# A gated mix of two attentions: every score and maxima product on 30 rows, and a re-spread order of the local work

## The chip, the core and the metric

The kernel runs on one core of one Trainium2 chip. Its engines are the TensorE (PE in the profile, with its weight loads shown apart as PEld), the VectorE (DVE), the ScalarE (ACT), GpSimd (POOL) and the SyncE (SP), which issues nearly all DMAs. Each engine takes its instructions in the order in which the program wrote them. The metric is the device time of one execution in microseconds; a time given for a kernel is the median of its runs.

## The reference

The input `x` has 2048 rows of 448 numbers; there are 16 heads of 28 numbers each. Two attentions are computed from the same `x`, with weights of their own, and mixed row by row with a gate.

```python
g = _sigmoid((x * gate_w).sum(-1, keepdims=True))
# A: each position looks at itself and at 7 earlier ones, 2 apart
idx = pos[:, None] - off[None, :]                  # off = arange(8) * 2
logits = jnp.einsum("bhsd,bhswd->bhsw", q, kg) * scale
logits = jnp.where(mask[None, None, :, :], logits, -1e9)
attn = _softmax(logits, axis=-1)
o = jnp.einsum("bhsw,bhswd->bhsd", attn, vg)       # then @ wo
# B: full attention
scores = jnp.einsum("bhqd,bhkd->bhqk", q, k) * (Dh ** -0.5)
p = _softmax(scores, axis=-1)
o = jnp.einsum("bhqk,bhkd->bhqd", p, v)            # then @ wo
return g * a + (1 - g) * b
```

A is called the local attention below, B the full one.

## The kernel before

Products that need more precision than one rounded operand gives are made of three: each operand is held as a rounded high part and a low part (the rest), and high by high, high by low and low by high are summed in PSUM.

**Stages.** First the projections: q, k and v of both attentions, with the q and k of the full one stored to DRAM as high and low parts (`qk_hi`, `qk_lo`). Then the main loop, 256 steps. A step is numbered `st = 16 * u + kt`: `u` runs over 16 units (4 groups of 4 heads, by 4 blocks of 512 queries), `kt` over 16 tiles of 128 keys. Last the output projection.

**Tiles of the scores.** `KH` and `KL` hold the high and low part of the keys of one group, `QH` and `QL` those of the queries of one unit. The four heads of a group lie at partitions 0, 32, 64 and 96, 28 rows each, so that the products of four heads use four row groups of the array. Under the 28 rows of `QH` lie two more that hold minus the row maximum (its high and low part); `KH` was filled with ones at the start, so a product over 30 rows gives the score with its maximum already taken off. The products with a low part, `KH` by `QL` and `KL` by `QH`, use 28 rows.

**A step** (`scores`, L1016 to L1060, in the list `WITH`): for each of the four heads three products of 512 columns (term 0: `KH` by `QH` on 30 rows; term 1: `KH` by `QL`; term 2: `KL` by `QH`), 12 in all at L1042. Between them stand up to three products s0, s1, s2 at L149 (28 rows), which are the scores of a coming unit with the queries as stationary operand; the DVE takes their maxima over the keys (L155: one reduction of 512 columns for s0, one of 1024 for s1 and s2). These maxima are used up after step 234; the last 21 steps have 12 products (`ALONE`). Two exponentials a step (L1047, ACT, 128x1024) turn the scores into `P`, and eight products (L1008, `av`) add `P` by `V` of the step before.

**The banks.** Three pairs of PSUM banks rotate through a step: one for heads 1 and 2, one for heads 3 and 0, one for s1 and s2. The pair that s1 and s2 of a step wrote, and that the second maxima reduction reads, is in the next step the pair of heads 3 and 0. So the product called 30 below (head 3, term 0) waits for the second reduction of the step before.

**The local attention** is worked off beside the main loop in 8 chunks, from four lists of items (`item`, `issue`): POOL multiplies and adds, DVE reduces (L663 for the scores, L674 and L684 for maximum and sum, L687 the reciprocal, L720 the transposition of the result), ACT takes one exponential for each chunk (L679), SP loads and stores. What a step takes of them is set by a budget: `late[engine]` grows by the cost of each item taken and falls by `step`, the assumed length of a step in microseconds, after each. For the DVE it also grows by 0.6 for each maxima product. An item is taken when what it needs was issued some steps before and the budget is not over its limit; the DVE takes at most two small instructions a step.

**Other work with a fixed place in a unit:** `osb` (L905) copies the finished `av` out, `onhi` (L943) rounds a finished unit's output, at the start of the step with kt 15 for most units and of kt 0 and 2 for the first. These stand ahead of that step's exponentials in ACT's order; the local exponential stands behind them.

Of the kernel before, what the change touches and what calls it, by code (L numbers as in the profile page):

```python
# [8 lines left out]
F32 = mybir.dt.float32  # L9
F32R = mybir.dt.float32r  # L10
# [5 lines left out]
S, D, H, DH = 2048, 448, 16, 28  # L16
NB, NJ, NG = 4, 16, 4
W, DIL = 8, 2
HALO = (W - 1) * DIL
SCALE = DH ** -0.5  # L20
NU = NG * NB
NMX = 192
# [3 lines left out]
def gated_mix_kernel(ctx: ExitStack, tc: tile.TileContext, xT, xn, gw, wA, wB, woAB, out):  # L26
    nc = tc.nc
# [3 lines left out]
    qk_hi = dram.tile([2 * D, S], F32R, name="qk_hi")  # L31
    qk_lo = dram.tile([2 * D, S], F32R, name="qk_lo")
# [42 lines left out]

    QP = [[cp.tile([128, 512], F32R, name=f"QP{i}{k}") for k in range(2)] for i in range(2)]

    def init_kh(t):
        nc.gpsimd.memset(t.bitcast(F32), 1.0)

    def pair(name):
        return pp.tile([128, 2, 512], F32, tag="P", name=name)

    half = {}
# [16 lines left out]
            r = D + 112 * g + DH * h  # L105
            dma_r(t[32 * h:32 * h + DH, c], src[r:r + DH, c])

    def load_part(u, name, src):
        g, b = divmod(u, NB)
        t = sp.tile([128, 512], F32R, name=name)  # L110
        for h in range(4):
            r = 112 * g + DH * h
            dma_r(t[32 * h:32 * h + DH, :], src[r:r + DH, 512 * b:512 * b + 512])
        return t

    Qs = {}

    def load_q(u, low=True):
        Qs[u] = load_part(u, "QH", qk_hi), load_part(u, "QL", qk_lo)
        if low:  # L120
            load_nm(u)

# [18 lines left out]
    def s1_mm(n, bank, half=False):  # L141
        u, i = divmod(n, 64)
        qs, kc, h = i // 16, i // 4 % 4, i % 4
        if u == 0:
            qs, kc = i // 8 % 4, 2 * (i // 32) + i // 4 % 2
        if i == 0 and u + 1 < NU:
            load_qhi(u + 1)
        r = slice(64 * (h // 2), 64 * (h // 2) + 64) if half else slice(32 * h, 32 * h + DH)
        nc.tensor.matmul(bank, qhis[u][h % 2][r, 128 * qs:128 * qs + 128],  # L149
                         KH[u // NB % 3][r, 512 * kc:512 * kc + 512], start=True, stop=True)  # L150

# [56 lines left out]

    for t in KH:
        init_kh(t)  # L210
    t0 = pair("t0")[:, 0, :]
    nc.vector.memset(t0, 0.0)
    nc.vector.memset(zt, 0.0)
    nc.vector.memset(omt, 0.0)

    zero = nc.const_aps.tensor(0.0, [128, 512], F32).bitcast(F32R)

# [391 lines left out]
    def main_tiles():  # L609
        nonlocal mp, pm, maskt, actx, a1, a2, a3  # L610
        hctx.close()
        mp = ctx.enter_context(tc.tile_pool(name="mp", bufs=1))

        KH.append(mp.tile([128, S], F32R, name="KH2"))
        KL.append(mp.tile([128, S], F32R, name="KL1"))
        init_kh(KH[2])
        pm = ctx.enter_context(tc.tile_pool(name="pm", bufs=8))

        maskt = mp.tile([128, W, NJ, 2], F32, name="maskt")
        nc.gpsimd.memset(maskt, 0.0)  # L620
        for st, g, t, src in ((12, 2, KH[2], qk_hi), (30, 1, KL[1], qk_lo), (72, 2, KL[0], qk_lo),
                              (100, 3, KH[0], qk_hi), (136, 3, KL[1], qk_lo)):
            at("end", st, lambda g=g, t=t, src=src: load_k(g, t, src))
        for w in range(1, W):
            nc.gpsimd.memset(maskt[0:1, w, 0:DIL * w, :], -1e9 / SCALE)

        actx = ExitStack()
        a1 = actx.enter_context(tc.tile_pool(name="a1", bufs=1))
        a2 = actx.enter_context(tc.tile_pool(name="a2", bufs=2))
        a3 = actx.enter_context(tc.tile_pool(name="a3", bufs=5))  # L630
        for nme in ("k", "v"):
            for i in range(2):
                t = a1.tile([128, HALO + NJ, 56], F32, name=f"{nme}t{i}")
                kvt[nme, i] = t
# [155 lines left out]
    def issue(eng, st, limit):  # L790
        q = lists[eng]
        i = 0
        while i < min(len(q), LOOK):
            if eng == "dve" and small.get(st, 0) >= 2:
                return
            key, name, cost, needs, f = q[i]
            if any(d in names and issued.get(d, 10 ** 6) + lag > st for d, lag in needs):
                i += 1
                continue
            if eng in late:  # L800
                if late[eng] + cost > limit:
                    return
                late[eng] += cost
            counted(f) if eng == "dve" else f()
            issued[name] = st
            q.pop(i)
            i = 0
# [211 lines left out]
    def scores(u, kt, cur):  # L1019
# [9 lines left out]
        for tok in WITH if k else ALONE:  # L1029
# [8 lines left out]
                continue  # L1038
            a, t = tok[0], int(tok[1])
            h = (int(a) + n) % 4  # L1040
            r = slice(32 * h, 32 * h + (DH + 2 if t == 0 else DH))
            nc.tensor.matmul(bank[a], (KH[g % 3], KH[g % 3], KL[g % 2])[t][r, ks], (qh, ql, qh)[t][r, :], start=(t == 0), stop=(t == 2))  # L1042
            if t == 2 and a in "20":
                if len(exps) < 5:
# [12 lines left out]
    for u in range(NU):  # L1057
        g, b = divmod(u, NB)
        for kt in range(NJ):
# [29 lines left out]
                at("dve", st + lag, lambda t=t, w=turned: w.update(r=counted(lambda: max_turn(t))))  # L1089
                at("end", st + lag, lambda v=v, w=turned: max_store(v, w["r"]))  # L1090
            issue("dve", st, DLIM)
            issue("act", st, 0)
            run("act", st)
            if prev is not None:
                do_av(prev)
# [6 lines left out]
                accs.extend((ring[0][:, 0, :], ring[1][:, 0, :]))  # L1102
                op_mm(0, accs[0], (0, 1, 2), first=True)
            run("end", st)
            step = 2.2 if left else 2.1
            late["dve"] = max(0.0, late["dve"] + 0.6 * min(3, left) - step)
            late["pool"] = max(0.0, late["pool"] - step)
    do_av(prev)
# [33 lines left out]
```

## Time and profile before

| | |
|---|---|
| median of 3 runs | 896.43 us (896.38 to 896.9) |
| the profiled execution's own time | 896.69 us |
| its span, first to last instruction | 894.9 us |
| granted TensorE clock over the span | 1.000 |
| busy: PE, DVE, ACT, POOL | 890.2, 740.5, 642.4, 638.7 us |
| projections, to the main loop | 0 to 248.4 us |
| main loop | 248.4 to about 824 us |
| output projection | from 821.4 us, 71 us to the end |

The stretches follow from where the first instruction at L1042 and the first at L886 stand. Durations of the engines overlap: an instruction can begin about a tenth of a microsecond before the one ahead of it has ended, so busy time divided by the span overstates how full DVE and ACT are. The end of a matmul is modelled, so its start is the surer number, and the distance between the starts of two matmuls of one row group is what is read below.

### The profile page before, as it was taken

To read this page: it belongs to the slowest core of one execution; us is meant where nothing else is said; L and a number is where in the kernel's file an instruction comes from. 1 tells how busy PE (TensorE), PEld (TensorE's weight loads), DVE (VectorE), ACT (ScalarE), POOL (GpSimd) and SP (SyncE) were. 2 spreads that over 40 slices of the span, in tenths; PEclk is the share of its full clock that TensorE was granted. 3 is DMA by queue.
4 is the path that set the end of the run, shared out by engine and by line. 5 is a ranking of instruction groups with operands and counts; after the bars stand their busy time and mean duration, and the time that the engine had idled before them with its cause. 6 is when DMAs were issued, how large, how long until landed. Compare 5 with 4: busy or idle time off the path is not lost.

```text
span 894.9 us, 20516 instructions
## 1 busy us (share of the span) xinstructions
PE 890.2 (99%) x8312; PEld 533.4 (60%) x8312; DVE 740.5 (83%) x962; ACT 642.4 (72%) x766; POOL 638.7 (71%) x505
## 2 busy tenths in 40 slices
PE   9999999999999999999999999999999999999998
PEld 7889999999954444444444444444444444434997
DVE  6688999999979999999999999999999999832220
ACT  7456434343378898898988989989888898897220
POOL 1499846464459789998999989999999799701000
PEclk9999999999999999999999999999999999999999
DMA  8886403454372241225225222533121322437781
GB/s 267 277 267 186 151 12 84 135 142 121 103 248 66 89 139 46 67 61 156 71 56 143 86 62 86 128 96 98 45 64 32 89 43 49 104 78 214 192 265 52
DMA packets 114038, 104.51 MB, mean 117 GB/s; under 512 B 75240, under 2 KB 82280, under 8 KB 113160
## 3 DMA queue, kind: packets, MB, share of 16 engines
q1 hardware_dynamic: 113512, 102.42, 40.7%
q8 instruction: 65, 1.06, 0.5%
q10 hardware_dynamic: 432, 0.79, 0.3%
q14 instruction: 29, 0.24, 0.1%
HBM read 62.20 MB, written 40.96 MB: 115 GB/s over the span
## 4 chain that ended last, share of the span: by engine, by line
PE 99%; ACT 0%; issue 0%; ACTq 0%
PE T L1042 31%; PE av L1008 28%; PE r L325 15%; PE r L320 8%; PE T L886 8%; PE r L149 4%; PE T L149 4%; PE r L220 0%; PE av L472 0%; ACT P L1047 0%; ACT res L895 0%; ACT onhi L943 0%; ACT L L679 0%; ACTq L943 0%
## 5 line engine op out<-in xcount | busy, mean ns | idle before, releaser
L1047 ACT ACTIVATE P<-T 128x1024 f32<-128x1024 f32 x512 | 496.8, 1023 | 59.6 <-PE T L1042 57.9
L155 DVE TENSOR_REDUCE MX<-T 128x1 f32<-128x512 f32 x470 | 442.5, 954 | 31.7 <-PE T L149 13.7
L1008 PE MATMUL av<-P,V 128*32 128x512 f32 x2048 | 272.7, 605 | 0.0
L1042 PEld LDWEIGHTS T<-QH,KH 30*128 30x128 f32 x1024 | 92.2, 181 | 229.1 <-ACT P L1047 196.5
L149 PE MATMUL T<-KH,QP 28*128 28x512 f32 x704 | 220.3, 456 | 0.1
L1042 PE MATMUL T<-QH,KH 30*128 30x512 f32 x1024 | 211.7, 489 | 0.2 <-ACT P L1047 0.2
L171 DVE TENSOR_REDUCE MX<-r 128x2 f32<-128x1024 f32 x160 | 192.9, 1221 | 20.1 <-PE r L149 16.3
L1042 PE MATMUL T<-QH,KL 28*128 28x512 f32 x1024 | 185.7, 393 | 0.0
L1042 PE MATMUL T<-QL,KH 28*128 28x512 f32 x1024 | 184.3, 392 | 0.0
L653 POOL TENSOR_TENSOR prod<-qt,kt 128x896 f32<-128x896 f32 x64 | 135.4, 2116 | 6.4 <-DMA kt<-a_scr 6.4
L397 ACT ACTIVATE raw<-r 128x896 f32<-128x896 f32 (+1 forms) x62 | 57.1, 921 | 94.5 <-PE r L325 91.9
L149 PE MATMUL r<-KH,QP 64*128 64x512 f32 x320 | 114.5, 391 | 0.0
L714 POOL TENSOR_TENSOR oat<-oat,prod 128x896 f32<-128x896 f32 x48 | 101.2, 2109 | 2.0
L149 PEld LDWEIGHTS T<-KH,QP 28*128 28x128 f32 x704 | 86.1, 181 | 26.7 <-ACT P L1047 17.7
L325 PE MATMUL r<-wh,xh 64*128 64x448 f32 (+1 forms) x504 | 99.6, 363 | 0.0
L709 POOL TENSOR_TENSOR prod<-vt,L 128x896 f32<-128x896 f32 x56 | 95.3, 1702 | 0.3
L398 POOL TENSOR_TENSOR ast<-raw 128x448 f32<-128x448 f32 x47 | 54.3, 1154 | 56.4 <-ACT raw L397 43.9
L1042 PEld LDWEIGHTS T<-QL,KH 28*128 28x128 f32 x1024 | 94.3, 185 | 0.0
L1042 PEld LDWEIGHTS T<-QH,KL 28*128 28x128 f32 x1024 | 93.3, 183 | 0.2
L1008 PEld LDWEIGHTS av<-P,V 128*32 128x32 f32 x2048 | 40.3, 107 | 77.9 <-issue 65.4
L325 PE MATMUL r<-wl,xh 64*128 64x448 f32 (+1 forms) x441 | 79.0, 365 | 0.0
L325 PEld LDWEIGHTS r<-wh,xh 64*128 64x128 f32 x504 | 77.9, 185 | 0.1
(122 smaller groups left out, 1138.8 us busy)
## 6 DMA issues: line engine op xcount, KB each, us to landing
a_scr<-ast SPq DMA_DIRECT2D x24, 448.0 KB
qk_hi<-qkh SPq DMA_DIRECT2D x24, 256.0 KB
qk_lo<-qkh SPq DMA_DIRECT2D x24, 256.0 KB
rbc<-rs SPq DMA_DIRECT2D x64, 64.0 KB
QP<-qk_hi SPq DMA_DIRECT2D x64, 56.0 KB
KL<-qk_lo SPq DMA_DIRECT2D x16, 224.0 KB
QH<-qk_hi SPq DMA_DIRECT2D x64, 56.0 KB
QL<-qk_lo SPq DMA_DIRECT2D x64, 56.0 KB
```

The costliest lines, as they stand in the source:

```text
L149: nc.tensor.matmul(bank, qhis[u][h % 2][r, 128 * qs:128 * qs + 128], KH[u // NB % 3][r, 512 * kc:512 * kc + 512], start=True, stop=True)
L155: i = nc.vector.tensor_reduce(MX[:, n % NMX:n % NMX + k], bank, axis=X, op=ALU.max)
L171: nc.vector.tensor_reduce(m, PM[k], axis=X, op=ALU.max)
L320: nc.tensor.matmul(bank, ws[c][rows, k, t[4]:t[4] + 128], x, start=first, stop=last)
L325: nc.tensor.matmul(bank[:, 0:cols], x, ws[c][rows, k, 0:cols], start=first, stop=last)
L653: nc.gpsimd.tensor_tensor(out=p, in0=qt[c], in1=kvt["k", c % 2][:, HALO - DIL * w:HALO - DIL * w + NJ, :], op=ALU.mult)
L709: nc.gpsimd.tensor_tensor(out=dst.rearrange("p j (h d) -> p j h d", d=DH), in0=kvt["v", c % 2][:, HALO - DIL * w:HALO - DIL * w + NJ, :].r ...
L714: nc.gpsimd.tensor_tensor(out=ows[c % 2][:, :, 0:56] if w == W - 1 else oat[c], in0=oat[c], in1=oat[c, w], op=ALU.add)
L886: writes(bank, nc.tensor.matmul(bank[:, :D], src, wo[c][k], start=(first and k == ks[0] and i == 0), stop=(last and k == ks[-1] and i == 2)))
L1008: nc.tensor.matmul(av[32 * h:32 * h + 32, :], V[:, kt, 4 * g + h, :], tiles_[h], start=(kt == 0), stop=(kt == NJ - 1), skip_group_check=True)
L1042: nc.tensor.matmul(bank[a], (KH[g % 3], KH[g % 3], KL[g % 2])[t][r, ks], (qh, ql, qh)[t][r, :], start=(t == 0), stop=(t == 2))
L1047: e = nc.scalar.activation(p, one if a == "2" else mine, AF.Exp, scale=SCALE).ins
```

## The change

Five edits, shown in the diff. `ROWS` is 30. The products of terms 1 and 2 at L1042 and the maxima products at L149 that used 28 rows now use 30. So that the two added rows give nothing, `KL` is filled with zeros at the start (POOL), and `QL`, which was a tile of a rotating pool, becomes two fixed tiles filled with zeros (DVE); the added rows of `QP`, the queries of the maxima products, are zeros already. Loads into these tiles write the same 28 rows of each head as before.

In the order of the local work, `step` goes from 2.2 to 2.17 while there are maxima products, and the local exponential is not taken in steps with kt 14 or 0.

```diff
+ROWS = DH + 2
...
+    QL = [cp.tile([128, 512], F32R, name=f"QL{i}") for i in range(2)]
     QP = [[cp.tile([128, 512], F32R, name=f"QP{i}{k}") for k in range(2)] for i in range(2)]
...
+    def init_kl(t):
+        nc.gpsimd.memset(t.bitcast(F32), 0.0)
...
-    def load_part(u, name, src):
+    def load_part(u, t, src):
         g, b = divmod(u, NB)
-        t = sp.tile([128, 512], F32R, name=name)
...
-        Qs[u] = load_part(u, "QH", qk_hi), load_part(u, "QL", qk_lo)
+        Qs[u] = load_part(u, sp.tile([128, 512], F32R, name="QH"), qk_hi), load_part(u, QL[u % 2], qk_lo)
...
-        r = slice(64 * (h // 2), 64 * (h // 2) + 64) if half else slice(32 * h, 32 * h + DH)
+        r = slice(64 * (h // 2), 64 * (h // 2) + 64) if half else slice(32 * h, 32 * h + ROWS)
...
+    init_kl(KL[0])
     t0 = pair("t0")[:, 0, :]
     nc.vector.memset(t0, 0.0)
     nc.vector.memset(zt, 0.0)
     nc.vector.memset(omt, 0.0)
+    for t in QL:
+        nc.vector.memset(t.bitcast(F32), 0.0)
...
         init_kh(KH[2])
+        init_kl(KL[1])
...
-            r = slice(32 * h, 32 * h + (DH + 2 if t == 0 else DH))
+            r = slice(32 * h, 32 * h + ROWS)
...
-            issue("act", st, 0)
+            if kt not in (NJ - 2, 0):
+                issue("act", st, 0)
...
-            step = 2.2 if left else 2.1
+            step = 2.17 if left else 2.1
```

On PE no product is added, removed or moved; the numbers of the loads and stores on SP are the same. DVE gains two fills, POOL two. Three places where the order changes:

The DVE in the main loop, steps 156 to 158 (`MX<-T` 128x1 and 128x2 are the two maxima reductions of a step, `L<-prod` the reductions of local scores); before:

```order
L155 TENSOR_REDUCE MX<-T_3245 128x1
L155 TENSOR_REDUCE MX<-T_3237 128x2
L663 TENSOR_REDUCE L<-prod 128x16 x2
L155 TENSOR_REDUCE MX<-T_3245 128x1
L155 TENSOR_REDUCE MX<-T_3233 128x2
```

and now:

```order
L159 TENSOR_REDUCE MX<-T_3249 128x1
L159 TENSOR_REDUCE MX<-T_3241 128x2
L159 TENSOR_REDUCE MX<-T_3249 128x1
L159 TENSOR_REDUCE MX<-T_3237 128x2
L671 TENSOR_REDUCE L<-prod 128x16 x2
```

The pair of local reductions moved one step on. Of the first 233 steps, 68 had no small DVE instruction behind their maxima, 98 had one and 67 two; now it is 61, 112 and 60. All the small instructions that stood among steps with maxima products stand there still.

ACT around steps 110 to 113 (`P<-T` are the exponentials, `onhi<-on` and `osb<-av` the work with a fixed place, `L<-L` the local exponential); before:

```order
L1047 ACTIVATE P<-T_3237 128x1024
L679 ACTIVATE L<-L 128x256
L943 ACTIVATE onhi<-on 128x512
L1047 ACTIVATE P<-T_3241 128x1024
L1047 ACTIVATE P<-T_3233 128x1024
```

and now:

```order
L951 ACTIVATE onhi<-on 128x512
L1055 ACTIVATE P<-T_3245 128x1024
L1055 ACTIVATE P<-T_3237 128x1024
...
L1055 ACTIVATE P<-T_3241 128x1024
L913 ACTIVATE osb<-av 128x512
...
L687 ACTIVATE L<-L 128x256
```

The local exponential of this chunk stands two steps later, no longer right ahead of a rounding. That of the first chunk goes the other way: it stood a step ahead of the first half of a rounding and now stands right ahead of it, at the turn from step 31 to 32.

SP after the last maxima, steps 240 to 247 (`rs<-osb`, `fsum`, `rs<-finv`, `rbc` are the row sums of unit 14 going through DRAM, `oa_scr<-tw` the last chunk of the local result, `oar` its first load for the output projection); before:

```order
L726 DMA oa_scr<-tw 384x1x32
L910 DMA rs_14_82<-osb 4x512
L914 DMA fsum<-rs_14_82 128x16
L923 DMA rs_14_98<-finv 128x16
L928 DMA rbc<-rs_14_98 32x512 x4
L856 DMA oar<-oa_scr 128x512
```

and now:

```order
L918 DMA rs_14_82<-osb 4x512
L922 DMA fsum<-rs_14_82 128x16
L734 DMA oa_scr<-tw 512x1x32
L734 DMA oa_scr<-tw 384x1x32
...
L931 DMA rs_14_98<-finv 128x16
L734 DMA oa_scr<-tw 512x1x32
...
L936 DMA rbc<-rs_14_98 32x512 x4
L864 DMA oar<-oa_scr 128x512
```

Before, all eight stores stood ahead of `rs<-osb`; now four stand behind `fsum` and four behind `rs<-finv`.

## The prediction

> **What bounds the kernel now.** I read the page's span and chain first.
>
> ```profile
> span 894.9 us, 20516 instructions
> PE 99%; ACT 0%; issue 0%; ACTq 0%
> PE T L1042 31%; PE av L1008 28%; PE r L325 15%; PE r L320 8%; PE T L886 8%; PE r L149 4%; PE T L149 4%; PE r L220 0%; PE av L472 0%; ACT P L1047 0%; ACT res L895 0%; ACT onhi L943 0%; ACT L L679 0%; ACTq L943 0%
> ```
>
> The chain names PE almost throughout. That says little, since overlapping matmul durations leave no visible idle time. So I went to windows of the main loop, and to the row of the maxima reductions in the first of them, for the length of a step.
>
> ```profile
> 288.41:757.06 468.65, 468.46 (x4790) 195.23 (x4786) 443.90 (x635) 418.41 (x472) 433.41 (x306) 1.00 0.31 81
> 757.06:779.46 22.40, 22.40 (x236) 9.40 (x232) 19.35 (x23) 19.71 (x22) 19.67 (x12) 1.00 0.39 89
> L155 DVE TENSOR_REDUCE MX<-T 128x2 f32<-128x1024 f32 (+1 forms) x417 | 393.0, 955 | 24.5 <-PE T L149 10.4 <-PE T L1042 6.0
> ```
>
> The columns after the length are busy time (and instructions) of PE, PEld, DVE, ACT and POOL, the clock, and DMA. Two maxima reductions a step, 417 of them, make 208 steps in the first window: 468.65/208 = 2.253 us a step. The second holds ten steps at the end of the maxima: 2.240 us. DVE is busy 443.90/208 = 2.134 us a step in the first and 1.935 in the second, where there is next to no local work. So 0.199 us of local DVE work a step costs 0.013 us of step. The clock is 1.00 in both.
>
> Then two whole steps by the timeline, PE first, then PEld, then DVE.
>
> ```profile
> 579.18 0.50 PE L1042 MATMUL T<-QH,KH 30*128 30x512 f32 x2
> ...
> 579.41 0.49 PE L1042 MATMUL T<-QH,KH 30*128 30x512 f32 x1
> 579.51 0.40 PE L1042 MATMUL T<-QL,KH 28*128 28x512 f32 x2
> 579.53 0.39 PE L1042 MATMUL T<-QH,KH 30*128 30x512 f32 x1
> ...
> 579.75 0.40 PE L1042 MATMUL T<-QH,KL 28*128 28x512 f32 x2
> 579.76 0.39 PE L1042 MATMUL T<-QL,KH 28*128 28x512 f32 x1
> 579.98 0.41 PE L1042 MATMUL T<-QH,KL 28*128 28x512 f32 x1
> ...
> 580.32 1.06 PE L1008 MATMUL av<-P,V 128*32 128x512 f32 x8
> 581.32 0.50 PE L1042 MATMUL T<-QH,KH 30*128 30x512 f32 x2
> ...
> 581.71 0.50 PE L1042 MATMUL T<-QH,KH 30*128 30x512 f32 x2
> ...
> 582.05 0.40 PE L1042 MATMUL T<-QL,KH 28*128 28x512 f32 x2
> ...
> 582.28 0.41 PE L1042 MATMUL T<-QH,KL 28*128 28x512 f32 x2
> 582.62 1.06 PE L1008 MATMUL av<-P,V 128*32 128x512 f32 x8
> 583.61 0.50 PE L1042 MATMUL T<-QH,KH 30*128 30x512 f32 x2
> ```
>
> ```profile
> 579.41 0.18 PEld L1042 LDWEIGHTS T<-QH,KH 30*128 30x128 f32 x2
> 579.52 0.18 PEld L1042 LDWEIGHTS T<-QL,KH 28*128 28x128 f32 x1
> ...
> 581.71 0.18 PEld L1042 LDWEIGHTS T<-QH,KH 30*128 30x128 f32 x2
> ```
>
> ```profile
> 578.13 1.23 DVE L155 TENSOR_REDUCE MX<-T 128x2 f32<-128x1024 f32 x1
> ...
> 579.75 1.90 DVE L155 TENSOR_REDUCE MX<-T 128x1 f32<-128x512 f32 x2
> ```
>
> The two steps begin at 579.18 and 581.32, and take 2.14 and 2.29 us. What differs is when product 30 (head 3, term 0) may load its weights. The second reduction of the step before ends at 578.13 + 1.23 = 579.36, and the load comes at 579.41; a step later it ends at 579.75 + 1.90 = 581.65, and the load comes at 581.71. From product 30 on both steps run alike: 0.34 to term 1, 0.23 to term 2, 0.34 to `av`, 1.00 to the next step, 1.90 together. So a step is (end of the maxima reduction + 0.05 to 0.06, from the step's start) + 1.90: 0.23 + 1.91 and 0.39 + 1.90. PE sets the step together with the DVE reduction that frees product 30's banks. A step that begins late finds that reduction nearer its end, so lost time is half returned by the next; that is why local DVE work costs so little.
>
> **The rows.** The edit could pay only if a change from 28 to 30 rows inside a row group costs something, and the 0.34 beside the 0.23 looks like it: 0.33 to 0.34 follows the 30-row products at 579.18, 579.41 and 581.71, 0.23 a 28-row one. But the 30-row product at 579.53 is followed in its row group by the 28-row one at 579.76, after 0.23, the same as the 0.24 from the 28-row products at 579.51 to those at 579.75. What the slow cases share is a first product with duration 0.49 or 0.50: its weights are loaded only as it starts (579.41 beside 579.41, 581.71 beside 581.71). The one at 579.53 had its weights loaded 0.12 ahead and lasts 0.39. The difference, 0.11 us, is a weight load not hidden behind a wait, and the change leaves those waits where they are. A load lasts 0.18 with 30 rows and 0.18 with 28, a product with hidden load 0.39 with either. So 1024 + 1024 products at L1042 and 704 at L149 go to 30 rows at 0.00 each. Bounds: dearer by at most the 0.01 to which these rows are read, on the three products from product 30 to `av`, 0.03 x 234 = 7 us if the rounding hid the most each time, which I give no weight since 0.39 stands at both row counts; cheaper by at most 0.11 a step (below).
>
> [...]
>
> **The fills.** One fill of `QL`, 128x512, is like the one at 0.91 below, one of `KL` is half of the two of `KH`.
>
> ```profile
> 0.91 0.48 DVE L212 MEMSET t<- 128x512 f32 x1 [0.91 <-PEq L1134]
> 4.64 0.43 DVE L443 CAST xh<-V 128x512 fp32r<-128x512 f32 x1 [3.18 <-DMA V<-in_xT]
> 1.25 3.54 POOL L83 MEMSET KH<- 128x2048 f32 x2
> 30.26 2.00 POOL L235 TENSOR_TENSOR wl<-raw,wh 128x384 fp32r<-128x384 f32 x2 [25.47 <-ACT wh L234]
> 261.60 2.13 POOL L653 TENSOR_TENSOR prod<-qt,kt 128x896 f32<-128x896 f32 x1 [6.44 <-DMA kt<-a_scr]
> ```
>
> The two of `QL`, 0.96 us, go into DVE's wait of 3.18 for the first input; `KL0`, 1.77, into POOL's wait of 25.47; `KL1`, 1.77, into its wait of 6.44 at the start of the main loop. Cost 0; uncovered, all of them 4.5 us.
>
> **The local work.** Nothing of it leaves the steps with maxima: the same instructions, placed more evenly. All local DVE work together costs 0.013 x 234 = 3.0 us, so between -3.0 and +3.0 lies whatever a new placing can do. If the price hangs on the steps with two small instructions, which fall from 67 to 60, the gain is 3.0 x 7/67 = 0.3 us. I take that, near zero, because the sum of work is unchanged.
>
> **The exponentials.** One place shows the collision that the edit is about.
>
> ```profile
> 500.57 0.42 ACT L679 ACTIVATE L<-L 128x256 f32<-128x256 f32 x1
> 500.88 0.63 ACT L943 ACTIVATE onhi<-on 128x512 fp32r<-128x512 f32 x1
> 501.40 4.01 ACT L1047 ACTIVATE P<-T 128x1024 f32<-128x1024 f32 x4
> 500.02:502.47 2.45, 2.27 (x27) 0.94 (x23) 2.42 (x5) 2.45 (x5) 2.45 (x2) 1.00 0.25 29
> ```
>
> Local exponential and rounding stand together ahead of the scores' exponential, and the step takes 2.45 instead of 2.25: 0.2 us, removed once. In the changed order the first chunk's exponential now stands right ahead of half a rounding (256 columns instead of 512), so about 0.1 comes back. Net -0.1. With this edit and the last, the two ends are -3.1 and +3.1.
>
> **The tail.** The last local stores move behind the row sums on SP. What waits behind them is the load of the local result, and behind that the split that PE needs.
>
> ```profile
> 790.80 5.92 SPq L726 DMA_DIRECT2D oa_scr<-tw  x8
> ...
> 805.87 0.42 SPq L856 DMA_DIRECT2D oar<-oa_scr  x1
> 815.98 0.69 DVE L865 TENSOR_TENSOR oalo<-oar,oahi 128x512 fp32r<-128x512 f32 x1
> 821.40 0.67 PE L886 MATMUL T<-KH,oahi 128*128 128x448 f32 x2
> ```
>
> The third block's split ends at 815.98 + 0.69 = 816.67; PE begins with it and the blocks before at 821.40. The eight issues of 0.74 each could slip 4.7 us before anyone waits. Cost 0.
>
> **Sum.** 0 (rows) + 0 (fills) - 0.3 - 0.1 + 0 = -0.4 us: 896.3 for the profiled execution, whose own time of 896.69 is 1.8 over its span and 0.26 over the median of the runs shown; 896.0 as a median.
>
> **Rivals.**
>
> 1. The even placing earns the whole price of the local work: steps of 2.240 throughout, -3.0, and -0.1 on ACT: 893.3. For it: 98 to 112 steps with just one small instruction. Against: 60 of the 67 pairs remain, and a late reduction is half returned anyway.
>
> 2. The change of rows does cost the 0.11 that I put down to unhidden loads. Each step's chain has one, from product 30, and as many steps as have maxima products would lose it: 0.11 x 234 = 25.7, so 870.3. For it: every 0.33 or 0.34 between two score products in these steps does follow one of 30 rows. Against: 579.53 to 579.76.
>
> 3. Slower, by the tail. If the eight stores go only after the second trip of the row sums, the load of the local result comes as late as that trip plus 5.92 us of issues. It decides once that load slips by over 4.7 us beyond 805.87; a slip of 7 us, the 5.92 and the rest of a landing, would put 2.3 us on the forecast's 896.0: 898.3. For it: four stores now stand behind `rs<-finv`. Against: the row sums no longer wait for the eight stores, so that trip begins earlier.
>
> **Chances.** Forecast 0.56, rival 1 0.22, rival 2 0.08, rival 3 0.14. The forecast's own range is 894.8 to 897.2. The range for 8 in 10 reaches down past rival 1 and up to rival 3: 892.0 to 898.5; rival 2 and about half of rival 3 stay out. A difference within 0.2%, 1.8 us, counts as none, about what a measurement of this kernel can tell: rivals 1 and 2 are faster, 0.30; the forecast is the same, 0.56; rival 3 slower, 0.14.
>
> **What would show it.** Rows right: in the changed timeline 0.34 still follows every product whose load comes with its start, and 0.23 the others, though all have 30 rows; 0.23 in the former shows rival 2. Local work right: 2.25 a step over the same stretch; 2.24 is rival 1. Exponentials: the step at 500.02 near 2.25 and the one after step 31 about 0.1 longer. Fills: the waits before the first cast and the first local product shorter by 0.96 and 1.77. Tail: idle PE ahead of the first L894 product would show rival 3. I am wrong, beyond the rivals, if products on 30 rows take another time than 0.39 when their weights are there, or if a reduction of local scores now waits for POOL, which none does before.

## The result and the profile after

The change is slower: 900.25 us (898.48 to 901.17, 5 runs) against 896.47 for the kernel before, run beside it (896.38 to 896.94), a ratio of 1.0037 with a 95% interval of 1.0026 to 1.0048. Run again in a later job, it stood at 898.86 (896.71 to 900.84, 9 runs) against 896.76, ratio 1.0024 (1.0014 to 1.0034). So the loss is 2 to 4 us, 0.2 to 0.4%, and the change scatters over 2.7 and 4.1 us where the kernel before, run beside it, keeps within 0.7. The profiled execution of the change took 898.48 us with a span of 896.7, 1.8 more than before; it is the fastest of the first five, so it shows only a part of the loss.

The page's span and chain, as they were read first for the kernel before:

```profile
span 896.7 us, 20515 instructions
PE 95%; DMA 2%; SPq 2%; DVE 0%; ACT 0%; issue 0%
PE T L1050 29%; PE av L1016 27%; PE r L332 15%; PE r L327 8%; PE T L894 8%; PE T L153 4%; PE r L153 4%; DMA kt<-a_scr 1%; SPq L734 1%; SPq L105 1%; DMA V<-in_xT 0%; ACT P L1055 0%; PE av L479 0%; DVE xh L450 0%; DMA QH<-nm 0%
```

Before, the chain was PE for 99%. Now 4% of it are DMA and SP's queue, in names that were not in it: `kt<-a_scr` (a load of the local attention), L734 (the stores `oa_scr`), L105 (loads of queries), `QH<-nm` (the row maxima of the next unit), and `DVE xh L450`, the first cast of the program. These are what has to be explained.

The windows of the main loop, with the same columns as in the prediction; first the 208 steps and the ten behind them, then three single steps, 79, 159 and 111:

```profile
289.63:758.86 469.23, 467.72 (x4788) 194.89 (x4784) 443.56 (x632) 418.29 (x472) 424.87 (x301) 1.00 0.30 81
758.86:781.26 22.40, 22.40 (x233) 9.40 (x229) 20.48 (x27) 19.76 (x22) 21.17 (x14) 1.00 0.36 86
...
429.13:432.19 3.06, 2.26 (x29) 0.97 (x25) 2.86 (x6) 2.99 (x4) 2.98 (x3) 1.00 0.23 63
609.67:612.72 3.05, 2.34 (x28) 0.97 (x25) 2.62 (x5) 3.05 (x4) 2.97 (x3) 1.00 0.39 81
501.94:504.05 2.11, 2.11 (x27) 0.87 (x24) 1.99 (x4) 2.11 (x4) 2.11 (x2) 1.00 0.05 6
```

The stretch takes 0.58 longer than before, yet PE is busy 0.74 less: it stands idle 1.51 us, where it stood idle 0.19. The steps 79 and 159, each the last of a unit, take 3.06 and 3.05; before no step was longer than 2.46. Without their surplus over an ordinary 2.25 the stretch would be about 1.0 shorter than before. The last row is the step with the collision of exponentials (2.45 before): it now takes 2.11.

The stretch begins at 289.63 instead of 288.41, so 1.22 us were lost before it. The timeline from the start shows where: POOL's fills first, then DVE, then PE, and last PE's first real product in the kernel before.

```profile
1.25 3.54 POOL L85 MEMSET KH<- 128x2048 f32 x2
4.73 1.80 POOL L88 MEMSET KL<- 128x2048 f32 x1
```

```profile
1.51 1.03 DVE L221 MEMSET QL<- 128x512 f32 x2
4.48 2.34 DVE L450 CAST xh<-V 128x512 fp32r<-128x512 f32 x1 [1.94 <-DMA V<-in_xT]
```

```profile
0.77 4.60 PE L227 MATMUL r<-const-float32-0.0 128*128 128x512 f32 x10 [0.77 <-PEq L1143]
6.96 0.70 PE L327 MATMUL r<-xh,wh 128*128 128x512 f32 x2 [1.59 <-DVE xh L450]
```

```profile
5.22 0.71 PE L320 MATMUL r<-xh,wh 128*128 128x512 f32 x2
```

The two fills of `QL` went into DVE's wait, as forecast. The cast behind them took 0.43 before and takes 2.34 now. Read its end, not its start: before, POOL's last fill ended at 1.25 + 3.54 = 4.79 and the cast at 4.64 + 0.43 = 5.07, 0.28 later; now the last fill ends at 4.73 + 1.80 = 6.53 and the cast at 6.82, 0.29 later. The cast did not run beside that fill. It was held to its end, and PE's first real product, which was at 5.22 before, comes at 6.96. In all seven profiles with the third fill at the start, the cast ends at 6.81 or 6.82, wherever its record begins (4.48 to 4.72). What holds it no trace shows, and the recorded starts do not show the hold either: the cast's record begins at 4.48, ahead of the third fill's at 4.73, and its end still came behind that fill's.

The tail is as it was: from the start of step 240 to the end 105.53 us, before 105.56.

### The profile page after: what moved, and what is told of

Read it like the earlier page. It is cut to its first block, busy times and chain, and to the rows that moved or that the text cites. A ratio compares the mean times of both kernels' runs of the same rounds, so it can differ in the third digit from the quotient of the medians.

```text
span 896.7 us, 20515 instructions
## 1 busy us (share of the span) xinstructions
PE 889.1 (99%) x8312; PEld 532.8 (59%) x8312; DVE 748.5 (83%) x964; ACT 642.2 (72%) x766; POOL 642.9 (72%) x507
## 4 chain that ended last, share of the span: by engine, by line
PE 95%; DMA 2%; SPq 2%; DVE 0%; ACT 0%; issue 0%
PE T L1050 29%; PE av L1016 27%; PE r L332 15%; PE r L327 8%; PE T L894 8%; PE T L153 4%; PE r L153 4%; DMA kt<-a_scr 1%; SPq L734 1%; SPq L105 1%; DMA V<-in_xT 0%; ACT P L1055 0%; PE av L479 0%; DVE xh L450 0%; DMA QH<-nm 0%
## 5 line engine op out<-in xcount | busy, mean ns | idle before, releaser
L153 PE MATMUL T<-KH,QP 30*128 30x512 f32 x704 | 221.6, 460 | 0.1
L1050 PE MATMUL T<-QH,KL 30*128 30x512 f32 x1024 | 185.9, 393 | 0.0
L1050 PE MATMUL T<-QL,KH 30*128 30x512 f32 x1024 | 183.2, 388 | 0.0
L153 PEld LDWEIGHTS T<-KH,QP 30*128 30x128 f32 x704 | 86.1, 181 | 27.3 <-ACT P L1055 16.6
L1050 PEld LDWEIGHTS T<-QL,KH 30*128 30x128 f32 x1024 | 93.9, 184 | 0.0
L1050 PEld LDWEIGHTS T<-QH,KL 30*128 30x128 f32 x1024 | 93.0, 182 | 0.2
```

## The experiments

In the table, times are of the profiled executions, taken from the starts of the first score product of a step. "Loop" is step 2 to step 240 less the 534.84 of the kernel before; step 2 begins there at 254.51. "Against before" is the difference of the medians within one job, where both kernels ran on one chip.

| run | step 2 begins | step 79 | step 159 | loop | median | against before | ratio, 95% interval |
|---|---|---|---|---|---|---|---|
| the change | 255.82 | 3.06 | 3.05 | +0.49 | 900.25 | +3.78 | 1.0037 [1.0026, 1.0048] |
| e8_change_again | 257.22 | 2.15 | 2.96 | -0.54 | 898.86 | +2.10 | 1.0024 [1.0014, 1.0034] |
| e1_order_only | 254.28 | 2.70 | 2.79 | +0.61 | 897.67 | +0.96 | 1.0011 [1.0002, 1.0019] |
| e2_rows_only | 257.36 | 2.16 | 2.32 | -0.72 | 898.57 | +1.86 | 1.0014 [1.0005, 1.0023] |
| e3_fill_moved | 254.63 | 2.44 | 2.97 | -0.40 | 896.97 | +0.26 | 1.0003 [0.9994, 1.0011] |
| e4_early_load | 257.01 | 3.32 | 2.26 | -0.14 | 897.92 | +1.21 | 1.0009 [1.0000, 1.0018] |
| e5_rows_old_order | 255.69 | 2.14 | 2.31 | -0.82 | 896.13 | -0.63 | 0.9994 [0.9985, 1.0002] |
| e6_fill_and_loads | 254.60 | 7.18 | 2.22 | +6.08 | 902.67 | +5.91 | 1.0065 [1.0052, 1.0078] |
| e7_warm14 | 255.80 | 2.94 | 3.81 | +1.01 | 898.95 | +2.19 | 1.0024 [1.0013, 1.0034] |
| e9_rows_warm14 | 255.82 | 2.16 | 2.32 | -0.72 | 897.16 | +0.56 | 1.0006 [0.9998, 1.0015] |
| e10_fill_alone | 257.05 | 2.14 | 2.31 | -0.05 | 899.17 | +2.57 | 1.0022 [1.0013, 1.0031] |
| e11_step_alone | 254.79 | 2.65 | 2.96 | -0.42 | 896.54 | -0.06 | 1.0000 [0.9991, 1.0008] |
| e12_act_alone | 254.43 | 2.13 | 2.30 | -0.88 | 895.98 | -0.62 | 0.9997 [0.9988, 1.0006] |
| e13_keys_later | 254.42 | 2.15 | 2.77 | -0.79 | 896.31 | -0.37 | 0.9996 [0.9987, 1.0004] |
| e14_both_repairs | 254.67 | 2.16 | 2.28 | -1.21 | 895.59 | -1.09 | 0.9987 [0.9978, 0.9996] |

### Taking the change apart: e1 to e4

e1_order_only is the kernel before with the two edits of the order:

```diff
-            issue("act", st, 0)
+            if kt not in (NJ - 2, 0):
+                issue("act", st, 0)
...
-            step = 2.2 if left else 2.1
+            step = 2.17 if left else 2.1
```

> Only the two edits to the order of the local work, on the kernel before: 28 rows, no fills. Theory S (the order puts the loads of a unit's queries and maxima too late on SP at units 5 and 10; the fill of KL0 slows the first cast at the start; rows cost nothing): the main loop begins where it did before (step 2 at 254.5 us from the span's start, not 255.8), the steps ahead of units 5 and 10 take about 3.0 us, and the median is what the change loses without the start, 900.25 - 1.3 = 899.0, with runs spread over some 2 us. Rival R (30 rows cost something): within 0.5 us of 896.5.

Measured 897.67, +0.96: between the two theories. The long steps are there without any row edit (79: 2.70, 159: 2.79), and step 2 begins as before. So the order carries the long steps, but they cost less than half of the 2.5 that theory S gave them.

e2_rows_only is the rest: the change with these two edits undone.

> Only the rows and their fills: the order of the local work is that of the kernel before. Theory S: 896.5 + 1.3 for the fill at the start = 897.8, runs within 0.5 us of each other, no step ahead of a unit over 2.5 us, mean step of the main loop 2.25 as before. Rival R: 899 to 900, with a longer mean step.

Measured 898.57, above theory S and below rival R. No step is long in it (79 and 159 at 2.16 and 2.32), and its loop is 0.72 shorter than before; all of the loss lies ahead of step 2, which begins 2.85 late. The times fall into two groups: three executions at 897.19 to 897.29 with a mean granted clock of 1.000, eight at 898.47 to 898.81 with 0.997 or 0.998.

e3_fill_moved is the change with one fill put elsewhere, behind a small fill of `V` (POOL reaches it at 101 us):

```diff
-    init_kl(KL[0])
     t0 = pair("t0")[:, 0, :]
...
                 nc.gpsimd.memset(V[:, :, :, DH:], 1.0)
+                init_kl(KL[0])
```

> The change with the fill of KL0 moved from the start to the fill of V in the projections (POOL, tile 32). Theory S: the first cast takes 0.43 us again instead of 2.34, the first real product starts at 5.2 us instead of 7.0, and the median falls by 1.3 to 898.9. Rival P (the late start is the DVE's own fills of QL or a late input, not POOL's fill): no change, 900.2.

Measured 896.97, +0.26, better than either theory: the cast takes 0.43 again, step 2 begins at 254.63, and 1.8 to 3.5 us of the loss are gone. Where this fill stood is the larger part of it.

e4_early_load is the change with the loads of the next unit's queries and maxima two steps earlier:

```diff
-            if u + 2 < NU and kt == 12:
+            if u + 2 < NU and kt == 10:
                 load_q(u + 1)
```

> The change with each unit's queries and maxima loaded at kt 10 instead of 12, which puts them ahead of the local loads and stores on SP at units 5 and 10. Theory S: the steps ahead of units 5 and 10 fall from 3.05 to under 2.4 us, the last issue of the maxima's load stands over 3 us ahead of each unit, and the median falls by at least the 1.6 of the profile, to 897.0 to 898.6, with a spread under 1 us. Rival R: no change, 900.2.

Measured 897.92, within the range of theory S, but only half of what it expected came about: step 159 is mended (2.26), step 79 is not (3.32), and the times span 3.6 us instead of less than 1. At unit 5 the edit changed nothing in the order on SP: the key loads and the three local loads still stand ahead of the queries. So the loads that stand in the way differ at the two units. For step 159 the chain of waits of the change and SP's own timeline show them:

```profile
610.00 0.55 SPq L105
...
610.59 1.99 DMA QH<-nm
612.58 0.14 issue
612.72 0.46 PE T L1050
```

```profile
600.33 6.03 SPq L734 DMA_DIRECT2D oa_scr<-tw  x8
606.41 1.84 SPq L105 DMA_DIRECT2D QH<-qk_hi  x4
608.29 1.66 SPq L105 DMA_DIRECT2D QL<-qk_lo  x4
610.00 1.11 SPq L105 DMA_DIRECT2D QH<-nm  x2
```

PE starts unit 10 at 612.72, when the last row maxima have landed. Their issue was behind eight stores of the local result that take SP 6.03 us. In e4_early_load only four of the stores stand ahead, the maxima are issued at 608.46, and unit 10 starts at 613.27 without a wait:

```profile
601.68 3.13 SPq L734 DMA_DIRECT2D oa_scr<-tw  x4
...
608.46 1.12 SPq L105 DMA_DIRECT2D QH<-nm  x2
```

What PE waits for at unit 5 of e4_early_load is the same kind of load, the last row maxima:

```profile
430.97 0.55 SPq L105
...
431.56 1.87 DMA QH<-nm
433.44 0.14 issue
433.57 0.49 PE T L1050 x2
```

### The start: e5, e7, e9, e10

e5_rows_old_order has the rows and the zero rows alone, the fill moved as in e3, the order of before.

> The change without its two edits of the order (step 2.2, exponential steps allowed to carry local work) and with the zero fill of the first low-part key tile moved from the program's start to the tile where the ones of V are filled. What is left of the change is the 30 rows and the zero rows, with no stall that the traces tie to them. Theory S (rows cost nothing, and give 3.3 ns a step as the run with rows alone showed, 232 steps x 3.3 ns = 0.8; the whole loss of that run was the fill): 0.8 below the kernel before, 895.9 where that stands at 896.7, main loop from step 2 to step 240 0.7 shorter than before, step 2 at 254.5. Rival R (the row edit itself costs time somewhere outside the main loop, and the fill is only part of it): 897 or more, step 2 later than 255.

Measured 896.13, -0.63, and the loop 0.82 shorter: theory S, though the interval of the ratio reaches 1.0002. (Step 2 begins at 255.69 in its profiled execution, not at the 254.5 expected; that execution is the slowest of its eleven, 897.01, and the others end 0.4 to 1.3 earlier.)

e10_fill_alone is the kernel before and one fill:

```diff
     for t in KH:
         init_kh(t)
+    nc.gpsimd.memset(KL[0].bitcast(F32), 0.0)
```

> The kernel before with one instruction more: the zero fill of the first low-part key tile, behind the two fills that stand at the program's start on GpSimd. Products with 28 rows, the order of before, nothing else of the change. Theory S (that fill alone makes the loss of the run with rows alone): the first cast takes 2.1 to 2.4 instead of 0.43, step 2 begins at 255.8 or 257.2 instead of 254.5, times in two groups about 1.2 and 2.6 above before, median 898.0 to 899.4. Rival R (the zeroing of the two small tiles on VectorE or the rows have a share): the cast stays under 1.0, or the median is below 897.6.

Measured 899.17, +2.57: theory S, with 28 rows and the old order. The times again fall into groups: four executions at 897.93 to 898.00, about 1.4 above the kernel before, six at 899.17 to 899.46, 2.6 to 2.9 above, and one alone at 896.96. So one instruction of 1.80 us on an engine that had nothing to do costs 1.4 us by holding the cast, which makes PE's first product 1.74 late, and in most executions 1.2 to 1.5 more. That second part is PE's speed at the start. Two views of the windows there, first of e8_change_again, then of e9_rows_warm14:

```profile
5.20:7.00 1.80, 0.04 (x1) 0.07 (x1) 1.76 (x2) 0.94 (x2) 1.34 (x1) 1.00 1.06 322
7.00:9.00 2.00, 2.00 (x5) 1.39 (x6) 2.00 (x5) 1.45 (x4) 0.00 (x0) 0.56 0.85 193
9.00:11.00 2.00, 2.00 (x7) 1.56 (x6) 1.94 (x5) 1.56 (x5) 0.00 (x0) 0.59 0.76 227
```

```profile
5.20:7.00 1.80, 0.27 (x3) 0.07 (x1) 1.76 (x2) 0.94 (x2) 1.33 (x1) 1.00 1.03 312
7.00:9.00 2.00, 2.00 (x8) 1.41 (x9) 2.00 (x5) 1.75 (x5) 0.00 (x0) 1.00 0.78 190
9.00:11.00 2.00, 2.00 (x11) 1.60 (x10) 1.94 (x5) 1.27 (x4) 0.00 (x0) 1.00 0.88 248
```

PE stands nearly idle from 5.2 to 7.0 in both. Behind that stretch the granted clock is 0.56 and 0.59 in the first, and 10 products start in the 4 us from 7 to 11; in the second it is 1.00, and 16 start. With ten products the clock does not fall in every execution: in the profiled one of the change it stayed at 1.00. What differs between the two programs at that place is the number of products on zeros at PE's start, ten and 14:

```diff
-    warm(10)
+    warm(14)
```

e7_warm14 is the change with this edit, e9_rows_warm14 the rows alone in the old order with it.

> The change with 14 products on zeros at its start instead of 10, which takes TensorE to about 7.2 us, past the end of the slow cast. Nothing else differs. Theory S (two losses at the start: the cast held up by the fill, 1.3 to 1.8, and then the clock, which falls to half for some 3 us in most executions because TensorE stood idle): the cast still takes about 2.3, the granted clock stays at 1.0 from there on in all executions, step 2 begins at 255.8 to 256.1 in the profile, the times lie closer together, and the median is 0.5 to 1.3 below the change as it was (run beside it). Rival R (the clock does not depend on that idle stretch): the clock still falls to half in some executions and the median is not below the change's.

> The 30 rows and the zero rows in the order of before (as in the earlier run whose times fell into two groups, 897.2 with a mean granted clock of 1.000 and 898.5 to 898.8 with one of 0.997 or 0.998), with 14 products on zeros at the start instead of 10. No long step is in this order, so only the start is on trial. Theory S (the two groups come from the idle stretch of 1.6 to 2.3 ahead of the first real product, after which the clock falls to half for about 3 us): one group alone, 897.0 to 897.6, clock 1.000, median 1.0 to 1.4 below the earlier 898.57, step 2 at 255.8 to 256.1. Rival R (the two groups come from elsewhere, as the change with 14 products had no lower median than the change): both groups again, median 898 or more.

e9 is clear: all eleven times lie between 897.08 and 897.32, one group with a clock of 0.999 or 1.000, and the median is 1.41 below that of e2 (1.30 when each is taken against the kernel before in its own job). The two groups of e2 were PE's speed at the start, and with 14 products the slow one is gone. How they do it is not what was expected, though: in e9's profiled execution they end at 5.43, and PE stands idle for 1.53 all the same; only in e7's do they last to 6.80. e7 was a miss: its median is that of the change beside it (898.95 and 898.86). Its start is mended, step 2 at 255.80 against 257.22, but in its profiled execution the steps 79 and 159 took 2.94 and 3.81 against 2.15 and 2.96, 1.64 more in all, which gives the gain back. These two steps vary between executions by more than the effect looked for; the effect shows only in an order without them.

### The unit starts: e6, e11, e12, e13, e14

e6_fill_and_loads is e3 with the loads of the next unit four steps earlier:

```diff
-            if u + 2 < NU and kt == 12:
+            if u + 2 < NU and kt == (8 if u < 13 else 12):
                 load_q(u + 1)
```

> The whole change, with two repairs: the fill of the first low-part key tile moved as in the earlier run, and the loads of the next unit's queries and maxima issued four steps earlier (from the ninth of sixteen steps on, ahead of the next group's key loads; the last two units as they were). Theory S (the loss of the change is the fill at the start plus the late loads at units 5 and 10): steps 79 and 159 fall from about 3.0 to 2.3 or less, the main loop from step 2 to 240 is 1.0 or more shorter than before, median 895.4 to 896.0. Rival R (the long steps come from the local work that now stands there and not from the late loads): both steps stay at 2.9 or more and the median stays at 896.9 or above.

Measured 902.67, the slowest of all. Step 159 is mended (2.22), step 79 takes 7.18. The queries and maxima of unit 5 now stand ahead of the key loads and the local loads, but what stands behind these is later still, as the chain says:

```profile
425.01 6.90 DMA rbc<-rs
...
432.12 1.27 POOL on L942
433.42 0.63 ACT onhi L951
434.05 0.92 ACT P L1055
435.01 1.73 PE T L1050 x11
```

What PE waits for here is `rbc`, the broadcast of the last unit's row sums: POOL's `on` (L942) needs it, ACT's rounding `onhi` needs `on` and stands idle 4.92 us for it, and `onhi` stands ahead of the exponentials of step 79. Behind this wait the granted clock is 0.50 for 6.83 us (434.12 to 440.95), and steps 80 and 81 take 3.87 and 3.00 as well.

In the change itself the same broadcast is late and POOL waits 3.36 us for it, but PE does not: `on` ends at 429.53, and ACT begins `onhi` at 429.67, while its exponential before runs to 429.78. SP's timeline of the change at unit 5, then PE's first product of that unit:

```profile
415.44 1.63 SPq L105 DMA_DIRECT2D KL<-qk_lo  x4
417.11 0.37 SPq L650 DMA_DIRECT2D qt<-a_scr  x1
...
418.00 0.42 SPq L655 DMA_DIRECT2D kt<-a_scr  x1
418.47 3.59 SPq L936 DMA_DIRECT2D rbc<-rs  x4
423.49 4.20 SPq L105 DMA_DIRECT2D QH<-qk_hi  x4
427.73 1.67 SPq L105 DMA_DIRECT2D QL<-qk_lo  x4
429.44 1.11 SPq L105 DMA_DIRECT2D QH<-nm  x2
```

```profile
432.19 0.50 PE L1050 MATMUL T<-QH,KH 30*128 30x512 f32 x2 [0.80 <-ACT P L1055]
```

Four key loads of 224 KB and three loads of the local attention of 448, 448 and 392 KB, 2.2 MB, are issued within 3 us. In the chain of the change the last of them lands 9.36 us after its issue. Everything behind them is late: the four broadcasts take 3.59 us to issue, the four query loads 4.20, and the maxima of unit 5 are issued from 429.44 to 430.55, 1.6 us ahead of the unit's start. Before, the three local loads were issued from 408.53 to 409.42 and the key loads from 413.44 on, ahead of broadcasts that took 1.69 to issue, and the maxima from 423.43 on, 5.6 us ahead of their unit.

The row puts PE's wait of 0.80 down to an exponential, which ended at 432.13. It was the maxima: the last of them landed at 432.05, and PE begins 0.14 behind it, the same as behind the landing at 433.44 in e4 and at 612.58 at unit 10. In e1, e3, e7 and e11, too, unit 5 begins 0.14 behind that landing. The change run again (e8) reaches unit 5 later, since its main loop begins 1.40 later; its maxima land at 432.51, unit 5 begins at 432.65 without a wait, and step 79 takes 2.15.

e13_keys_later is e3 with the four key loads put off by twelve steps; e14_both_repairs adds the earlier loads of e4 for unit 10 alone:

```diff
-        for st, g, t, src in ((12, 2, KH[2], qk_hi), (30, 1, KL[1], qk_lo), (72, 2, KL[0], qk_lo),
+        for st, g, t, src in ((12, 2, KH[2], qk_hi), (30, 1, KL[1], qk_lo), (84, 2, KL[0], qk_lo),
...
-            if u + 2 < NU and kt == 12:
+            if u + 2 < NU and kt == (10 if u == 9 else 12):
                 load_q(u + 1)
```

> The change with the first fill moved (as in the earlier run with a median of 896.97) and one load moved: the four key loads of 224 KB that stand at step 72, right ahead of the three local loads of unit 5, go to step 84. Theory S (step 79 is long because those 0.9 MB and the 1.3 MB of the local loads fill the DMA engines to 427, so that the broadcasts, queries and maxima of unit 5 land late): the local loads land about 4 earlier, POOL's wait for the broadcasts at unit 5 (3.1 to 3.4) goes, steps 79 and 80 take 2.35 or less each; step 159 stays at 2.5 or more; the median falls by 0.2 to 0.6 below 896.97. Rival R (the local loads in front of the broadcasts do it alone, or the local work that stands there): step 79 stays above 2.4 and the median within 0.2.

> The kernel of the run above with one more edit: the queries and maxima of unit 10 are loaded two steps earlier, ahead of half of the eight stores. Theory S: steps 79 and 159 at 2.35 or less, main loop from step 2 to 240 0.9 to 1.4 shorter than before, median 895.3 to 896.0, so that the whole order of the change, once its late loads are mended, is no slower than the order of before with the same rows (896.13). Rival R (the new order loses elsewhere as well): median 896.4 or more.

With the key loads out of the burst the local loads still stand ahead of the broadcasts, and it is enough. SP's timeline of e13_keys_later, then the maxima in e3_fill_moved:

```profile
414.39 0.43 SPq L655 DMA_DIRECT2D kt<-a_scr  x1
414.93 1.76 SPq L936 DMA_DIRECT2D rbc<-rs  x4
...
422.44 1.11 SPq L105 DMA_DIRECT2D QH<-nm  x2
```

```profile
427.60 1.11 SPq L105 DMA_DIRECT2D QH<-nm  x2
```

The maxima are issued 5.2 us earlier than in e3, POOL's wait is gone, step 79 takes 2.15, step 159 as before its repair 2.77: theory S, with a gain of 0.63 against before (from +0.26 to -0.37), a little over what was expected; the intervals of the two ratios overlap, so it is the step, not the median, that shows it. e14 mends both, its loop is 1.21 shorter than before, and its median of 895.59 is below both kernels, 0.13% below the one before (the interval ends at 0.9996). Its eleven times span 0.56 us, those of the change 2.7 and 4.1. The late loads and the slow start are not all of that scatter: e12 below has neither in its profiled execution, and its times span 1.9. The row of e14's 208 steps:

```profile
288.45:755.99 467.54, 467.53 (x4789) 194.82 (x4786) 443.95 (x632) 418.49 (x472) 425.44 (x301) 1.00 0.30 81
```

e11_step_alone and e12_act_alone are e3 with only one of the two edits of the order, the step of 2.17 or the rule for the exponential.

> The change with the fill moved and without its rule for the exponentials: what is left is 30 rows and the step of 2.17 instead of 2.2. Its queue of SyncE is that of the change at units 5 and 10 (key loads directly ahead of the broadcasts and query loads, eight stores ahead of the query loads). Theory S (the step constant alone brings the late loads): steps 79 and 159 take 2.5 to 3.5, step 111 stays near 2.1 to 2.5, main loop from step 2 to 240 0.3 to 1.0 longer than with the old order (which was 1.0 shorter than before by the earlier run), median 896.3 to 897.2. Rival R (the exponential rule makes the long steps): 79 and 159 at 2.35 or less and the median at 896.1 or less.

> The change with the fill moved and with the old step of 2.2: what is left is 30 rows and the rule that keeps local work from the exponentials of two steps in sixteen. Its queue of SyncE has the key loads of unit 5 where before has them, and at unit 8 eight stores directly ahead of the query loads. Theory S (the rule takes away the collision of step 111, worth about 0.3, and the long steps belong to the step constant): step 111 at 2.2 or less, 79 and 159 at 2.35 or less, median 895.4 to 896.0, the best of all so far. Rival R (the rule carries the long steps, or unit 8 gets late in the same way): a step of 2.5 or more at 79, 127 or 159 and a median of 896.4 or more.

Theory S in both. The step constant alone brings the long steps (2.65 and 2.96). The rule alone takes the collision of step 111 away (2.17 instead of 2.46 in e5) and brings no long step, but its loop is only 0.06 shorter than that of e5; about half of the gain is given back at step 33 (2.33 instead of 2.18). The step constant alone also takes that collision away (2.13), so the change did not need the rule for it.

### The sum: e8

> The change itself once more, so that the other three stand beside it on one chip. Theory S: about 3 above the kernel before (898.5 to 901), steps 79 and 159 at 3.0. If the sum of the two parts run alone holds (the order alone 1.0 and the rows with the fill 1.9 above before), the median is 2.9 above before. Rival R (the parts interact): it is more than 1 away from that sum.

Measured +2.10, against a sum of 0.96 + 1.86 = 2.82 from e1 and e2; the first job had +3.78. From the later runs, all against before: the fill +2.57 (e10), the rows -0.63 (e5), the order +0.89 (e3 less e5), together +2.83, in the middle of the two measurements of the change. The order's +0.89 is +1.35 for the late loads (e3 less e14) and -0.46 for the rest of it (e14 less e5). Each of these medians is uncertain by about 0.8 us, so the fill and the late loads are clear of noise, and the -0.63 and the -0.46 are not.

## Why the prediction was wrong

It said 896.0 with no measurable difference, and the change is slower. Point by point:

- **The step that failed first: the fill of `KL0`.** The prediction put "`KL0`, 1.77, into POOL's wait of 25.47" at a cost of 0, and as the cost without cover 4.5 for all fills. The cover was there on POOL, and it was the wrong engine to ask. DVE's first cast, and with it PE's first product, stood right behind POOL's fills already before (the two rows quoted there, 4.79 and 5.07, show it), and a third fill holds it 1.75 longer. Shown by e3 and e10: +2.57, the largest term of all, about 1.4 of it the held cast and the rest PE's slower start behind it, for which the prediction had no term. The fills of `QL` and of `KL1` did go into the waits named for them: DVE's wait ahead of the cast shrank from 3.18 to 1.94, POOL's ahead of the first local product from 6.44 to 3.91, and e5, which still has these fills, is no slower for them.
- **The second: the local work.** "Nothing of it leaves the steps with maxima", and the gain was put at 0.3. Only the instructions of DVE and ACT were counted. The local work also has loads and stores in SP's queue, and at units 5 and 10 these came right ahead of the queries and maxima, and PE stood waiting for the last of the maxima. SP was read at the tail alone, in the third rival: the right mechanism at a place where it did not happen. Shown by e4, e13 and e14: +1.35. Once the loads are mended, the order gains 0.46, where -0.3 and -0.1 were forecast. The size agrees, but it is not clear of noise, and no run tests whether the steps with two small instructions carry it, so this agreement may be luck.
- **The rows** were right in mechanism. 0.34 still follows a product whose load came late, and 0.23 the others, with 30 rows everywhere. In step 79 of the change, PE's timeline, heads 3 and 0:

```profile
429.42 0.49 PE L1050 MATMUL T<-QH,KH 30*128 30x512 f32 x1
429.76 0.40 PE L1050 MATMUL T<-QL,KH 30*128 30x512 f32 x2
429.99 0.40 PE L1050 MATMUL T<-QH,KL 30*128 30x512 f32 x2
```

  The weights of the product at 429.42 are loaded at 429.42. From there to 429.76 is 0.34, and on to 429.99 it is 0.23. The second rival, 0.11 a step, is out. But 0.00 was not exact: with the order of before the 208 steps take 2.250 us each (467.95/208 in e5; 468.01 and 468.03 in e2 and e9) instead of 2.253 (468.65; 468.60 in e10), and the median of e5 is 0.63 lower. That is 3 ns a step, a third of the 10 ns to which single rows can be read.
- **The exponentials:** the step at 500.02 came down to 2.11 (2.25 was forecast), and the steps 32 and 33, behind the exponential that now stands right ahead of a rounding, grew from 2.31 and 2.19 to 2.36 and 2.40, 0.26 together where 0.1 was forecast. The net is the 0.06 of e12 against e5, of the size of the 0.1 but too small to tell from nothing.
- **The tail and the other rivals:** nothing changed from step 240 on, so the third rival did not come about; the first (2.240 a step) did not either.

## What to carry to other kernels

A new instruction is not free because its engine is idle (one fill of 1.80 us on POOL cost 2.57 in e10): look at which instruction of another engine begins or ends with that engine's present work, above all ahead of the first product of a program. Where a table or a budget spreads work anew, read the DMA queue at every place where a next stage is loaded, not only at the end, and add up the bytes that stand ahead of a small transfer that is waited for (here 2.2 MB ahead of the row maxima of unit 5, for which PE waited 0.80 us). An edit that looks slower can hold a gain: here two moved loads and one moved fill turned +2.1 to +3.8 us into -1.1.

## What was not expected of the hardware

The cast on DVE beside the third fill on POOL was not slowed but held: 0.43 us became 2.10 to 2.34, with its end 0.28 or 0.29 behind the third fill in each of the seven profiles that have it at the start.

PE starts slow, and the clock column does not show it. In every profile the first products on zeros start 0.43 apart, from the second on, while the column says 1.00. They come to 0.22 apart behind the seventh product in e9, behind the eighth in e8, and in the change not before the tenth and last. In the profiled execution of e10_fill_alone the first real products are still slow: the column says 1.00 from 7 to 9 us, while the first pairs start 0.99 and 0.85 apart (6.96, 7.95, 8.80) and those of e9 0.64 and 0.57. No idle stretch is needed for that: in e3 the first four real products come 0.42 to 0.56 apart right behind the products on zeros, and step 2 still begins at 254.63.

A fall of the clock in the column is a second thing. In e8 it reads 0.50 from 7.24 to 10.65 and in e2 from 7.76 to 11.17, 3.41 us each, behind idle stretches of 2.28 and 2.03. Behind the 1.59 of the change and the 1.53 of e9 it did not fall. In both falls the clock fell 3.41 us behind the point where PE's products had come to 0.22 apart (3.83 in e8, 4.35 in e2), and in these 3.41 us PE was busy for 1.13 and 1.38. In e9 that point is at about 3.55, and in the 3.41 us behind it PE was busy for 1.88. So it may be the busy share of such a stretch that decides, an estimate from these three traces, which are too few to show it; why 14 products suffice was not tried further.

A load of 392 KB took 9.36 us to land behind 1.8 MB issued just ahead of it. And where the 3 ns a step come from that the row edits save is open: no row of the profile is fine enough to show it, and no run parts the 30 rows from the two fixed tiles of `QL` that came with them.
